# Windowed attention and a gated MLP in one kernel: a new order for all steps, with GpSimd's loads placed anew

## The chip, the cores and the metric

The kernel runs on one core of a Trainium2 chip. The metric is the time of one execution in device microseconds; "before" is the median of three runs. An engine is named as the profile names it: PE (TensorE's matmuls, with PEld for its weight loads), DVE (VectorE), ACT (ScalarE), POOL (GpSimd), SP (SyncE). SPq and POOLq are the instructions with which SP and POOL start DMA transfers.

## What is computed

Two stages, one behind the other. The first is attention with a sliding window of 128 and four "sink" positions that every query sees; the second is a gMLP block over its result. Shapes: batch 4, 8 heads, sequence 768, head size 64; model width 512, hidden width 1024 (two halves of 512).

```
scores = q @ k^T / 8                               # per batch and head
keep   = (col < 4) | (0 <= row - col < 128)
a      = softmax(where(keep, scores, -1e9))
x      = (a @ v), heads side by side               # [4, 768, 512]
h      = gelu_tanh(x @ w_in);  u, v = halves of h
v_n    = (v - mean) / sqrt(var + 1e-6) * g_ln
v_s    = w_sg @ v_n (over the sequence) + b_sg
out    = x + (u * v_s) @ w_out                     # float32
```

## The kernel before

The four batches go through one after the other, and the attention of one batch is interleaved with the gMLP of the batch before it. Everything is cut into named steps, some 670 of them, and the string STEPS lists them in the order in which they are issued. Each engine, and each of the two DMA queues (SP's and POOL's), carries out its own instructions in exactly that order. A step waits only for the data and the buffers that it needs; so the list fixes, for every engine, who stands behind whom. The numbers behind a step's name are batch, head pair or tile group; a last letter D, A or P says which engine does the step (DVE, ACT, POOL).

The steps that matter here:

- **Loads of q, k, v.** Batch 0's q and k come by head pairs as float32 over SP's queue (LPQ, LPK: four pairs each, 393 KB each), are cast to bf16 by an engine (CPQ, CPK), and are transposed on PE (TQ, TK: 12 transposes each), with the result copied out of PSUM by EQ and EK. Batches 1 and 2 are loaded over POOL's queue with a cast in the DMA (LQ, LK, six tiles each, 128 KB as bf16) and transposed on PE as well; batch 3 is loaded the same way, but its transposes are DMA transposes on SP's queue (DQ, DK). v is loaded over POOL's queue in two halves of four heads (LVH, 384 KB as bf16 each). w_in comes in two halves (LW.0 for the v half, LW.1 for the u half, 512 KB as bf16), w_sg in two (LWS), w_out in one (LWO), all over POOL's queue.
- **Attention.** QK.b.p.g makes the scores of head pair p for two tiles of queries (g = 0, 1, 2; a fourth number means that the mask is added on PE with two more matmuls), EX takes exp on ACT, MK applies the mask (on DVE in one instruction, on POOL in two), SK and SX do the sink columns. AV.b.p.k multiplies with v, where batch 0 has k = 0, 1, 2 (two tiles each) and the others k = 0, 1 (three tiles each). NR divides by the row sums and writes x (x_sb).
- **gMLP.** x is transposed, for batch 0 on PE (XT, copied out by XE), for the others by DMA transposes on SP's queue (XD, half a batch each). MV is the v half of x @ w_in (8 matmuls of 512 columns), GV its gelu on ACT; MU and GU are the same for the u half. BN, RS, NM and Z are the normalization (RS, a power of -1/2, on POOL). WT and WE transpose w_sg once. SP is the product with w_sg (SP.b.hf.dc, six matmuls), GT scales and adds the bias, GM multiplies with u. OU is the product with w_out, RA adds x, ST and SH store over SP's queue. The very last tile goes in two column halves (OH, RH, SH).
- **Buffers.** PSUM has two score buffers (sc, used by QK, MV and MU in the order of the list) and four others (mm, used by TQ, TK, XT, AV, WT, SP, OU and so on). A step that takes a new buffer waits until the one that it used last (two or four allocations ago) has been read out.
- **Fillers.** HM.n puts n matmuls on zeros in front of the next step. TBL.E and TBL.G run an exp or a gelu on one column, so that ACT's table is loaded at that place rather than with the first real use.

Of the kernel before, what the change touches and what calls it, by code (L numbers as in the profile page):

```python
# [30 lines left out]
LK.1.4 NM.0.1 WE.0.A WT.1 GV.0.2 LK.1.5 TK.1.1 MU.0.2 LB.P EK.1.1.A BN.0.2 Z.0.0.A LK.2.0 WT.2 GU.0.2 MU.0.0 WE.1.D
RS.0.2 WE.2.D Z.0.1.A LQ.2.0 NM.0.2 Z.0.2.A Z.0.3.D Z.0.4.D WT.3 LQ.2.1 WT.4 GU.0.0 TBL.E WE.3.D WT.5 LQ.1.4 Z.0.5.D
TQ.1.1 QK.1.0.0 EQ.1.1.D QK.1.1.0 LQ.1.5 SP.0.0.0 WE.4.D LK.2.1 EX.1.0.0 VSM.1 SP.0.0.1 WE.5.D EX.1.1.0 LVH.1.0
GT.0.0.0 TK.1.2 KS.1 GT.0.0.1 QK.1.2.0 QK.1.3.0 EX.1.2.0 SP.0.0.2 LVH.1.1 GM.0.0.0.D EX.1.3.0 MK.1.2.0.D TQ.2.0
EK.1.2.A LQ.2.2 QK.1.0.1 EQ.2.0.D QK.1.1.1 TQ.1.2 EX.1.0.1 GT.0.0.2 LWO SP.0.0.3 EQ.1.2.D EX.1.1.1 LK.2.2 MK.1.0.1.D
TK.2.0 MK.1.0.0.D QK.1.2.1 LK.2.3 EK.2.0.A QK.1.3.1 MK.1.3.0.D SK.1.0 GM.0.0.1.D LQ.2.3 SP.0.1.0 EX.1.2.1 GT.0.0.3
MK.1.1.0.D LQ.2.4 EX.1.3.1 SP.0.1.1 MK.1.1.1.D LQ.2.5 MK.1.2.1.D SX.1.0 QK.1.0.2 QK.1.1.2 GT.0.1.0 EX.1.0.2 GM.0.0.2.P
SP.0.1.2 GT.0.1.1 EX.1.1.2 LK.2.4 GM.0.1.0.D AV.1.0.0 MK.1.3.1.D AV.1.1.0 LK.2.5 GM.0.0.3.D QK.1.2.2 GT.0.1.2 QK.1.3.2
EX.1.2.2 SP.0.1.3 NR.1.0.0 MK.1.1.2.P EX.1.3.2 NR.1.1.0 AV.1.2.0 AV.1.3.0 MK.1.0.2.P GT.0.1.3 QK.2.0.0 QK.2.1.0
NR.1.2.0 EX.2.0.0 OU.0.0 MK.1.2.2.P NR.1.3.0 TK.2.1 RA.0.0 AV.1.0.1 XD.1.0 EK.2.1.A MK.1.3.2.P AV.1.1.1 NR.1.0.1  # L40
AV.1.2.1 EX.2.1.0 GM.0.1.2.P NR.1.1.1 AV.1.3.1 NR.1.2.1 QK.2.2.0 LK.3.0 QK.2.3.0 EX.2.2.0 OU.0.1 NR.1.3.1 GM.0.1.3.P
EX.2.3.0 TBL.G OU.0.2 XD.1.1 RA.0.1 GM.0.1.1.P TK.2.2 MK.2.3.0.D TQ.2.1 LVH.2.0 TQ.2.2 EQ.2.1.D MV.1.0 EQ.2.2.D LQ.3.0
EK.2.2.D LQ.3.1 VSM.2 MU.1.0 GV.1.0 MK.2.1.0.D LVH.2.1 BN.1.0 MV.1.1 GU.1.0 LQ.3.2 RA.0.2 LQ.3.3 MK.2.0.0.D MV.1.2
GV.1.1 MK.2.2.0.D LK.3.1 KS.2 LK.3.2 BN.1.1 MU.1.1 GV.1.2 LK.3.3 BN.1.2 RS.1.1 MU.1.2 GU.1.1 LQ.3.4 NM.1.1 Z.1.0.A
RS.1.2 OU.0.3 GU.1.2 TBL.E LQ.3.5 NM.1.2 Z.1.1.D SK.2.0 Z.1.4.D QK.2.0.1 Z.1.2.D Z.1.3.A QK.2.1.1 Z.1.5.D OU.0.4
RA.0.3 DK.3.0 SP.1.0.0 RA.0.4 SX.2.0 EX.2.0.1 SP.1.0.1 GT.1.0.0 DQ.3.0 EX.2.1.1 GM.1.0.0.D SP.1.1.0 MK.2.0.1.P
GT.1.0.1 QK.2.2.1 ST.0.3 GT.1.1.0 QK.2.3.1 GM.1.0.1.P DQ.3.1 EX.2.2.1 AV.2.0.0 SP.1.1.1 MK.2.1.1.D EX.2.3.1 MK.2.2.1.P
NR.2.0.0 AV.2.1.0 QK.2.0.2 DQ.3.2 QK.2.1.2 KS.3 EX.2.0.2 MK.2.3.1.P NR.2.1.0 SP.1.1.2 GT.1.1.1 EX.2.1.2 OU.0.5
MK.2.0.2.P GT.1.1.2 ST.0.0 ST.0.4 QK.2.2.2 RA.0.5 QK.2.3.2 MK.2.1.2.P EX.2.2.2 AV.2.2.0 AV.2.3.0 NR.2.2.0 SP.1.1.3
EX.2.3.2 NR.2.3.0 QK.3.0.0 MK.2.3.2.P QK.3.1.0 GT.1.1.3 XD.2.0 EX.3.0.0 AV.2.0.1 MK.2.2.2.D AV.2.1.1 EX.3.1.0 NR.2.0.1  # L50
AV.2.2.1 GM.1.1.3.P ST.0.1 NR.2.1.1 AV.2.3.1 ST.0.2 ST.0.5 GM.1.1.0.P SK.3.0 NR.2.2.1 QK.3.2.0 QK.3.3.0 NR.2.3.1
EX.3.2.0 GM.1.1.2.P SP.1.0.2 EX.3.3.0 XD.2.1 SP.1.0.3 GT.1.0.2 SX.3.0 TBL.G MK.3.3.0.D MV.2.0 GM.1.0.2.P DK.3.1
GM.1.1.1.D LK.3.4 MK.3.0.0.D OU.1.3 LVH.3.0 GV.2.0 OU.1.4 RA.1.3 LVH.3.1 OU.1.5 ST.1.3 RA.1.4 GT.1.0.3 MV.2.1 ST.1.4
MK.3.1.0.D LK.3.5 BN.2.0 GM.1.0.3.P MV.2.2 GV.2.1 BN.2.1 MU.2.1 GV.2.2 BN.2.2 RS.2.1 MU.2.0 GU.2.1 NM.2.1 RA.1.5
RS.2.2 MU.2.2 GU.2.0 NM.2.2 Z.2.4.D Z.2.5.D Z.2.0.A Z.2.1.D OU.1.0 GU.2.2 TBL.E Z.2.2.D MK.3.2.0.D OU.1.1 RA.1.0
Z.2.3.D QK.3.0.1 QK.3.1.1 RA.1.1 SP.2.0.0 EX.3.0.1 DK.3.2 EX.3.1.1 OU.1.2 MK.3.0.1.P GT.2.0.0 ST.1.5 VSM.3 ST.1.0
QK.3.2.1 ST.1.1 QK.3.3.1 EX.3.2.1 SP.2.1.0 GM.2.0.0.D MK.3.1.1.P RA.1.2 EX.3.3.1 SP.2.0.1 ST.1.2 MK.3.3.1.P QK.3.0.2
GT.2.0.1 QK.3.1.2 EX.3.0.2 SP.2.1.1 GT.2.1.0 MK.3.2.1.P EX.3.1.2 GM.2.1.0.D SP.2.1.2 GT.2.1.1 GM.2.0.1.D AV.3.0.0
MK.3.1.2.P GT.2.1.2 AV.3.1.0 NR.3.0.0 AV.3.2.0 AV.3.3.0 MK.3.0.2.P NR.3.1.0 QK.3.2.2 QK.3.3.2 EX.3.2.2 SP.2.0.2
NR.3.2.0 NR.3.3.0 EX.3.3.2 TBL.G SP.2.0.3 MK.3.2.2.P GT.2.0.2 XD.3.0 AV.3.0.1 GT.2.0.3 MK.3.3.2.P AV.3.1.1 NR.3.0.1  # L60
AV.3.2.1 GM.2.0.3.P NR.3.1.1 AV.3.3.1 SP.2.1.3 GM.2.0.2.D GM.2.1.1.P NR.3.2.1 OU.2.0 NR.3.3.1 GT.2.1.3 XD.3.1 OU.2.1
RA.2.0 GM.2.1.3.P OU.2.2 GM.2.1.2.D SH.2.0.0 SH.2.0.1 RA.2.1 MV.3.0 RA.2.2 SH.2.1.0 SH.2.1.1 OU.2.3 GV.3.0 OU.2.4
BN.3.0 MV.3.1 RA.2.3 RA.2.4 MV.3.2 SH.2.3.0 SH.2.3.1 GV.3.1 SH.2.2.0 SH.2.2.1 SH.2.4.0 SH.2.4.1 BN.3.1 OU.2.5 GV.3.2
MU.3.2 BN.3.2 RS.3.1 MU.3.1 GU.3.2 NM.3.1 RS.3.2 NM.3.2 Z.3.0.D Z.3.1.A MU.3.0 Z.3.2.D Z.3.3.A Z.3.4.A Z.3.5.D RA.2.5
SH.2.5.0 SH.2.5.1 SP.3.1.0 GU.3.0 SP.3.1.1 GU.3.1 GT.3.1.0 SP.3.1.2 GM.3.1.0.D GT.3.1.1 SP.3.1.3 GM.3.1.1.D GT.3.1.2
# [650 lines left out]
```

## Time and profile before

| | |
|---|---|
| median of 3 runs | 155.65 us (155.44 to 155.72) |
| the profiled execution's own time | 155.89 us |
| its span, first to last instruction | 154.2 us |
| PE / DVE / ACT / POOL busy | 145.7 / 122.9 / 100.0 / 99.7 us |
| software DMA queue (POOL's) | 64608 packets, 11.01 MB, 95.7% of 16 engines' span |
| hardware DMA queue (SP's) | 22552 packets, 13.41 MB, 33.0% |
| granted TensorE clock | 1.0 throughout |

Times in the views are microseconds from the start of the span. A PE that is shown busy need not be at its peak, since matmuls are pipelined and their ends are modelled. The share of a DMA queue adds up its packets' times, and packets of one engine overlap, so a share can pass 100% in a short window. Packets and bytes per microsecond say more.

### The profile page before, as it was taken

What the parts mean: (1) busy time and instruction counts of PE and PEld (TensorE: products, weight loads), DVE (VectorE), ACT (ScalarE), POOL (GpSimd) and SP (SyncE); (2) the same over time, 40 slices, a digit from 0 to 9 for tenths busy, and PEclk for the clock granted to TensorE, in tenths of its full rate; (3) what the DMA queues carried; (4) which work ended last, traced back from release to release, by engine and by line L of the source; (5) the groups of instructions that cost most, each with busy time, mean ns of one, the idle gap of its engine ahead of it and who ended that gap; (6) DMA issues with size and microseconds to landing.
All of it is one profiled execution on the core that took longest, in us unless ns stands there. A gap on an engine that the chain in (4) does not pass through costs nothing.

```text
span 154.2 us, 3867 instructions
## 1 busy us (share of the span) xinstructions
PE 145.7 (95%) x1540; PEld 94.5 (61%) x1554; DVE 122.9 (80%) x296; ACT 100.0 (65%) x117; POOL 99.7 (65%) x127
## 2 busy tenths in 40 slices
...
GB/s 158 305 351 157 154 195 204 166 189 211 148 141 154 185 155 140 147 150 156 156 223 250 81 276 177 185 190 81 211 72 1 105 221 73 150 54 20 0 203 206
DMA packets 87178, 24.67 MB, mean 160 GB/s; under 512 B 78772, under 2 KB 84920, under 8 KB 87160
## 3 DMA queue, kind: packets, MB, share of 16 engines
q0 software_dynamic: 64608, 11.01, 95.7%
q1 hardware_dynamic: 22552, 13.41, 33.0%
...
## 4 chain that ended last, share of the span: by engine, by line
PE 54%; POOL 18%; DMA 15%; ACT 4%; DVE 4%; issue 2%; SPq 1%; DVEq 0%; ACTq 0%; POOLq 0%
PE mm L627 15%; DMA v_sb<-in_v_dram 11%; PE mm L644 10%; PE sc L566 9%; PE sc L607 8%; POOL q L225 5%; POOL k L225 4%; DMA uT<-in_k_dram 4%; PE sc L483 4%; PE mm L524 3%; POOL v_sb L271 3%; PE mm L528 2%; POOL wsg_gated L637 2%; POOL P L498 2%; POOL P L501 2%
## 5 line engine op out<-in xcount | busy, mean ns | idle before, releaser
L488 ACT ACTIVATE P<-sc 128x1024 bf16<-128x1024 f32 (+1 forms) x48 | 43.4, 952 | 10.3 <-PE sc L483 10.1
L627 PE MATMUL mm<-wsgT,z 128*128 128x384 bf16 x192 | 34.4, 327 | 0.3 <-ACT z L597 0.3
L627 PEld LDWEIGHTS <-z 128*128 128x128 bf16 x192 | 17.6, 98 | 12.5 <-issue 0.7
L570 ACT ACTIVATE vt<-sc 128x1024 f32<-128x1024 f32 x12 | 12.3, 1027 | 18.4 <-PE sc L566 18.4
L632 DVE SCALAR_TENSOR_TENSOR gtmp<-mm,g_sb,b_bc 128x384 bf16<-128x384 f32 x32 | 19.0, 610 | 4.2 <-PE mm L627 4.0
L637 POOL TENSOR_TENSOR wsg_gated<-gtmp,uT 128x384 bf16<-128x384 bf16 x15 | 14.9, 1006 | 11.3 <-DVE gtmp L632 11.2
L607 PE MATMUL sc<-xT,w_in_sb 128*128 128x256 bf16 x192 | 22.1, 273 | 0.0
L566 PE MATMUL sc<-w_in_sb,xT 128*128 128x512 bf16 x92 | 21.8, 379 | 0.2
L644 PE MATMUL mm<-w_out_sb,wsg_gated 128*128 128x512 bf16 x85 | 21.2, 379 | 0.5
L498 POOL TENSOR_SCALAR_AFFINE_SELECT P<-P 128x512 bf16<-128x512 bf16 x21 | 13.7, 653 | 11.4 <-ACT P L488 11.4
L607 PEld LDWEIGHTS <-w_in_sb 128*128 128x128 bf16 x192 | 18.7, 98 | 2.9
L579 DVE BATCH_NORM_STATS2 st<-vt 128x6 f32<-128x512 f32 x24 | 15.4, 685 | 6.1 <-ACT vt L570 6.0
L541 DVE TENSOR_TENSOR x_sb<-mm,rcp 128x384 bf16<-128x384 f32 (+1 forms) x36 | 18.5, 513 | 1.2
L588 POOL TENSOR_TENSOR rs<-rs,neg_half 128x4 f32<-128x4 f32 (+1 forms) x8 | 7.1, 882 | 15.8 <-DVE rs L583 14.4
L225 POOL DMA_DIRECT2D k<-in_k_dram x18 | 16.4, 924 | 1.3 <-DMA v_sb<-in_v_dram 1.3
L648 DVE TENSOR_TENSOR ot<-mm,x_sb 128x512 f32<-128x512 f32 x23 | 15.4, 683 | 2.2 <-PE mm L644 2.2
L225 POOL DMA_DIRECT2D q<-in_q_dram x18 | 16.8, 956 | 0.0
L524 PE MATMUL mm<-v_sb,P 128*128 128x65 bf16 x192 | 16.1, 194 | 0.6 <-DVE x_sb L541 0.4
L524 PEld LDWEIGHTS <-P 128*128 128x128 bf16 x192 | 14.5, 97 | 2.5 <-DMA v_sb<-in_v_dram 0.6
L528 PE MATMUL mm<-v_sb,P 128*128 128x65 bf16 x160 | 15.4, 193 | 0.4 <-POOL P L501 0.4
L612 ACT ACTIVATE uT<-sc 128x1024 bf16<-128x1024 f32 x12 | 12.2, 1024 | 5.1 <-PE sc L607 5.1
L566 PEld LDWEIGHTS <-xT 128*128 128x128 bf16 x96 | 9.2, 98 | 10.1
...
## 6 DMA issues: line engine op xcount, KB each, us to landing
...
```

Of the source, the lines that this page charges most:

```text
L225: return nc.gpsimd.dma_start(out=dst.rearrange("p (h d) -> p h d", h=H), in_=heads(src, b, i))
L488: nc.scalar.activation(out=P.new((b, p, g))[:, :, 0:w], in_=sc_ring[b, p, g][:, :, 0:w], func=AF.Exp, scale=scale)
L498: nc.gpsimd.affine_select(out=p4[:, :, :, 0:128], in_=p4[:, :, :, 0:128], compare_op=ALU.is_ge, fill=0.0, base=0, pattern=[[0, 2], [0, 2], ...
L524: nc.tensor.matmul(av[:, il, hl, :], pt[:, hl, c:c + 128], vb[:, h, i, :], start=first, stop=False)
L528: nc.tensor.matmul(av[:, il, hl, :], pt[:, hl, c:c + 128], vb[:, h, i - 1, :], start=False, stop=(i < 2 and il == n - 1 and hl == 1))
L541: nc.vector.tensor_mul(x_sb.get(b)[:, i0:i0 + n, 128 * p:128 * (p + 1)].rearrange("p t (h d) -> p t h d", h=2), av[:, :, :, 0:Dh], rcp[:, ...
L566: nc.tensor.matmul(hp[:, jl, :], xT[b][:, 2 * g + jl, c, :], w_in_sb[:, c, d_half:2 * d_half], start=(c == 0), stop=(c == KD - 1))
L607: nc.tensor.matmul(hp[:, dc // 2, 256 * (dc % 2):256 * (dc % 2 + 1)], w_in_sb[:, c, 128 * dc:128 * (dc + 1)], xT[b][:, 2 * g:2 * g + 2, c, :],
L627: nc.tensor.matmul(ps[:, 0:NH], z[b][:, si, 128 * dc:128 * (dc + 1)], wsgT[:, si, NH * hf:NH * (hf + 1)], start=(si == 0), stop=(si == NT ...
L632: nc.vector.scalar_tensor_tensor(out=gtmp.new((b, hf, dc)), in0=mm_ring["g", b, hf, dc][:, 0:NH], scalar=g_sb[:, dc:dc + 1], in1=b_bc[:, N ...
L637: (nc.vector if e == "D" else nc.gpsimd).tensor_mul(gated(b, hf)[:, dc, :], gtmp[b, hf, dc], uT[b][:, dc, NH * hf:NH * (hf + 1)])
L644: nc.tensor.matmul(ps, gated(b, hf)[:, dc, 128 * tl:128 * (tl + 1)], w_out_sb[:, dc, :], start=(dc == 0), stop=(dc == KU - 1))
```

## The change

STEPS is written in a new order from its first step to its last. The steps are the same, with these exceptions and notes:

- Some steps change the engine. From ACT to DVE go CPQ.0, CPK.2, XE.0.1, XE.0.2, EK.0.1, EK.0.3, EK.1.0, EK.1.1, EK.1.2, EK.2.1, EQ.0.2, WE.0 and a few Z; from DVE to ACT EQ.0.0, EQ.0.1, EQ.0.3, EQ.1.2, GCP, WE.1 and some Z; CPK.1 goes from POOL to DVE and CPQ.3 from DVE to POOL; masks and GM steps are dealt anew between DVE and POOL (MK.0.2.2 and MK.0.3.2 go to POOL).
- On POOL's queue, v of batch 0 is issued behind the masks' set-up, in front of all casts; then come two q tiles of batch 1 and both halves of w_in (with CPQ.3.P between the halves), half of w_sg, and then the rest.
- The order of the pair loads on SP's queue becomes q0, k0, k1, q1, q2, q3, k2, k3.
- Fillers: 19 matmuls instead of 21.
- TBL gets a second argument that it doesn't use; its seven calls stand in other places (TBL.G.2 in front of EX.2.2.0; TBL.E.1 and TBL.E.2 behind the first exps of their stretch; TBL.G.3, TBL.E.3 and TBL.G.4 at the end).
- OH.3.5.1 is issued before OH.3.5.0, for which OH takes its buffer with whichever half comes first.

The start of the list, where most of the prediction's steps lie:

```diff
-WARM LPQ.0 FILL LPK.0 LPK.1 LPQ.1 LPQ.2 LG MASK LPK.2 LPK.3 CPQ.0.A VSK LPQ.3 IDEN CPK.0.A IDEN2 MASK0 HM.9 TQ.0.0
-TK.0.0 EQ.0.0.D EK.0.0.A VSO HM.4 QK.0.0.0 ZERO CPK.1.P QK.0.0.1.1 EX.0.0.0 LVH.0.0 EX.0.0.1 QK.0.0.2.1 CPQ.1.D TK.0.1
-EX.0.0.2 LC CPQ.2.D LVH.0.1 TQ.0.1 MK.0.0.0.D EK.0.1.A HM.1 TQ.0.2 EQ.0.1.D EQ.0.2.A HM.3 QK.0.1.0 CPK.2.A CPK.3.P
-QK.0.1.1.1 EX.0.1.0 LQ.1.0 CPQ.3.D TK.0.2 EX.0.1.1 TK.0.3 EK.0.2.D LQ.1.1 TQ.0.3 EK.0.3.A GTR EQ.0.3.D LW.0 HM.1
-QK.0.2.0 QK.0.2.1 EX.0.2.0 LK.1.0 KS.0 VSM.0 HM.3 SK.0.2 EX.0.2.1 SK.0.1 MK.0.2.0.D AV.0.0.0 LW.1 QK.0.3.0.1
...
-MK.0.1.2.P QK.0.3.2 AV.0.3.1 EQ.1.0.A NR.0.2.1 XT.0.0 NR.0.3.1 LWS.0 AV.0.0.2 EX.0.3.2 TBL.G AV.0.1.2 XE.0.0.D LK.1.1
-XT.0.1 MK.0.2.2.D MV.0.0 XE.0.1.A LK.1.2 NR.0.0.2 MK.0.3.2.D LK.1.3 NR.0.1.2 AV.0.2.2 AV.0.3.2 LQ.1.2 NR.0.2.2 GV.0.0
...
+WARM ZERO FILL IDEN MASK LPQ.0 LPK.0 MASK0 CPQ.0.D LPK.1 LVH.0.0 IDEN2 LVH.0.1 CPK.1.D CPK.0.A LPQ.1 HM.7 TQ.0.0 HM.3
+TK.0.0 EQ.0.0.A EK.0.0.A HM.4 QK.0.0.0 LPQ.2 LPQ.3 TK.0.1 LQ.1.0 LQ.1.1 LG LW.0 QK.0.0.1.1 CPQ.1.D EK.0.1.D CPQ.2.D
+TQ.0.1 EX.0.0.0 VSK EX.0.0.1 EQ.0.1.A CPQ.3.P QK.0.0.2.1 LPK.2 LW.1 LPK.3 EX.0.0.2 VSO LWS.0 MK.0.0.0.D CPK.3.P
+QK.0.1.1.1 TQ.0.2 CPK.2.D EQ.0.2.D QK.0.1.0 EX.0.1.1 TK.0.2 TQ.0.3 EX.0.1.0 LC LK.1.3 TK.0.3 EK.0.2.D QK.0.2.0
+EQ.0.3.A EX.0.2.0 QK.0.2.1 EX.0.2.1 EK.0.3.D KS.0 MK.0.1.0.D HM.3 SK.0.1 SX.0.1 VSM.0 QK.0.3.0.1 QK.0.3.1 EX.0.3.0
+EX.0.3.1 MK.0.3.1.P SK.0.2 HM.1 AV.0.1.0 AV.0.1.1 AV.0.0.1 MK.0.2.1.D QK.0.1.2 MK.0.2.0.D NR.0.1.0 QK.0.3.2 SX.0.2
+AV.0.0.0 GTR NR.0.1.1 EX.0.1.2 GCP.A NR.0.0.1 HM.1 AV.0.3.0 AV.0.2.1 NR.0.0.0 NR.0.3.0 MK.0.1.2.P NR.0.2.1 QK.0.2.2
+AV.0.2.0 AV.0.3.1 EX.0.3.2 AV.0.0.2 NR.0.2.0 NR.0.3.1 TQ.1.0 NR.0.0.2 EX.0.2.2 XT.0.0 MK.0.3.2.P MK.0.2.2.P XT.0.1
+XE.0.0.D EQ.1.0.A XE.0.1.D AV.0.1.2 NR.0.1.2 AV.0.3.2 LK.1.1 AV.0.2.2 MV.0.0 MV.0.1 TBL.G.1 NR.0.3.2 LK.1.0 GV.0.0
```

And the places of the later batches that the prediction speaks of, as they stand in the new list:

```
MK.1.3.2.P LK.3.0 LQ.2.5 GM.0.1.2.P EX.2.0.0 QK.2.1.0 NR.1.0.1 GM.0.1.0.P NR.1.2.0 LVH.2.0 NR.1.3.0 OU.0.0 AV.1.2.1
RA.0.0 AV.1.1.1 NR.1.2.1 EX.2.1.0 OU.0.1 AV.1.3.1 QK.2.2.0 NR.1.1.1 RA.0.1 LQ.3.1 LQ.3.0 QK.2.3.0 LQ.3.4 XD.1.0
GM.0.1.1.D GM.0.1.3.D TK.2.2 NR.1.3.1 MK.2.1.0.D TQ.2.1 OU.0.2 TBL.G.2 EX.2.2.0 EK.2.2.D LQ.3.5 TK.2.1 LK.3.1 XD.1.1
RA.0.2 EX.2.3.0 VSM.2 MV.1.0 GV.1.0 MU.1.0 EK.2.1.D MK.2.2.0.D BN.1.0 MV.1.1 GU.1.0 LQ.3.3 DK.3.0 MK.2.0.0.D MV.1.2
...
MK.2.3.1.D AV.2.2.0 AV.2.0.0 LK.3.3 GT.1.1.0 NR.2.2.0 NR.2.0.0 GM.1.1.0.P MK.2.1.2.P AV.2.1.0 SP.1.1.2 AV.2.3.0
...
GM.1.1.2.P ST.0.0 NR.2.3.1 XD.2.0 QK.3.3.0 EX.3.2.0 SP.1.0.3 EX.3.3.0 MV.2.0 OU.1.3 XD.2.1 MV.2.1 GT.1.0.2 GV.2.0
...
GT.3.0.0 GM.3.1.1.P GT.3.1.3 SP.3.1.2 GT.3.1.2 GM.3.1.2.D SH.2.0.0 GM.3.1.3.D GM.3.0.3.P SH.2.5.1 SP.3.0.1 GM.3.0.0.P
OU.3.3 GT.3.0.1 GM.3.0.1.D SH.2.4.1 RA.3.3 OU.3.4 RA.3.4 OU.3.0 ST.3.3 OU.3.1 TBL.G.3 TBL.E.3 OU.3.2 RA.3.0 OH.3.5.1
RA.3.1 OH.3.5.0 ST.3.4 RA.3.2 RH.3.5.0 RH.3.5.1 ST.3.0 ST.3.1 ST.3.2 SH.3.5.0 SH.3.5.1 TBL.G.4
```

```diff
-    def TBL(func):
+    def TBL(func, turn):
...
-        ps = mm_ring["o", b, t] if h else fresh(mm_ring, ("o", b, t))
+        ps = mm_ring["o", b, t] if ("o", b, t) in mm_ring.held else fresh(mm_ring, ("o", b, t))
```

More of the change, by code (lines that the diff above doesn't have):

```diff
@@ L26 @@
-MK.0.1.0.D SX.0.1 SX.0.2 QK.0.3.1 MK.0.2.1.P GCP.D NR.0.0.0 EX.0.3.0 AV.0.0.1 AV.0.1.0 AV.0.1.1 NR.0.0.1 EX.0.3.1
-QK.0.1.2 NR.0.1.0 AV.0.2.0 AV.0.3.0 EX.0.1.2 MK.0.3.1.P NR.0.1.1 QK.0.2.2 AV.0.2.1 NR.0.2.0 EX.0.2.2 TQ.1.0 NR.0.3.0
-MK.0.1.2.P QK.0.3.2 AV.0.3.1 EQ.1.0.A NR.0.2.1 XT.0.0 NR.0.3.1 LWS.0 AV.0.0.2 EX.0.3.2 TBL.G AV.0.1.2 XE.0.0.D LK.1.1
-XT.0.1 MK.0.2.2.D MV.0.0 XE.0.1.A LK.1.2 NR.0.0.2 MK.0.3.2.D LK.1.3 NR.0.1.2 AV.0.2.2 AV.0.3.2 LQ.1.2 NR.0.2.2 GV.0.0
-MV.0.1 NR.0.3.2 LQ.1.3 BN.0.0 LWS.1 XT.0.2 GV.0.1 MU.0.1 XE.0.2.A BN.0.1 WT.0 GU.0.1 TK.1.0 MV.0.2 RS.0.1 EK.1.0.A
@@ L31 @@
[L31 to L65, printed above, removed]
@@ L66 @@
-SP.3.0.0 GM.3.1.2.D SP.3.0.1 GT.3.0.0 GT.3.1.3 SP.3.0.2 GT.3.0.1 GM.3.1.3.P SP.3.0.3 GM.3.0.0.D GM.3.0.1.P GT.3.0.2
-OU.3.3 GM.3.0.2.D GT.3.0.3 OU.3.4 GM.3.0.3.D RA.3.3 OU.3.0 RA.3.4 ST.3.3 OU.3.1 RA.3.0 ST.3.4 OU.3.2 ST.3.0 RA.3.1
-OH.3.5.0 OH.3.5.1 ST.3.1 RA.3.2 ST.3.2 RH.3.5.0 SH.3.5.0 RH.3.5.1 SH.3.5.1
+WARM ZERO FILL IDEN MASK LPQ.0 LPK.0 MASK0 CPQ.0.D LPK.1 LVH.0.0 IDEN2 LVH.0.1 CPK.1.D CPK.0.A LPQ.1 HM.7 TQ.0.0 HM.3
+TK.0.0 EQ.0.0.A EK.0.0.A HM.4 QK.0.0.0 LPQ.2 LPQ.3 TK.0.1 LQ.1.0 LQ.1.1 LG LW.0 QK.0.0.1.1 CPQ.1.D EK.0.1.D CPQ.2.D
@@ new lines @@
+AV.0.2.0 AV.0.3.1 EX.0.3.2 AV.0.0.2 NR.0.2.0 NR.0.3.1 TQ.1.0 NR.0.0.2 EX.0.2.2 XT.0.0 MK.0.3.2.P MK.0.2.2.P XT.0.1
+XE.0.0.D EQ.1.0.A XE.0.1.D AV.0.1.2 NR.0.1.2 AV.0.3.2 LK.1.1 AV.0.2.2 MV.0.0 MV.0.1 TBL.G.1 NR.0.3.2 LK.1.0 GV.0.0
+LK.1.2 NR.0.2.2 XT.0.2 MU.0.1 LWS.1 VSM.1 GV.0.1 LQ.1.3 GU.0.1 BN.0.0 XE.0.2.D MV.0.2 WT.0 MU.0.2 BN.0.1 WE.0.D GV.0.2
+LQ.1.2 LB.P TK.1.0 RS.0.1 LQ.1.5 NM.0.1 BN.0.2 WT.1 Z.0.3.A LQ.2.0 LK.1.4 Z.0.2.A MU.0.0 Z.0.1.D WT.2 WT.3 EK.1.0.D
+Z.0.0.D RS.0.2 GU.0.2 TK.1.1 QK.1.0.0 NM.0.2 Z.0.4.D WE.2.D Z.0.5.D LQ.2.1 LQ.1.4 WE.1.A KS.1 GU.0.0 WE.3.D QK.1.1.0
```

27 lines of the change are left out of this document (added).

## The prediction

> **What bounds the kernel now.** I read the busy times by stage first, then the DMA queues, then the timeline of the stage that the change rebuilds most.
>
> The windows, in microseconds from the span's start: length, then busy time of each engine.
>
> ```profile
> 0.00:16.50 16.50, 14.05 (x165) 7.01 (x169) 10.20 (x31) 12.41 (x15) 10.47 (x19) 1.00 1.36 236
> ...
> 23.40:76.00 52.60, 51.29 (x568) 36.01 (x571) 43.49 (x107) 41.64 (x50) 46.65 (x53) 1.00 2.01 165
> 76.00:150.50 74.50, 73.92 (x674) 46.14 (x678) 62.65 (x139) 39.35 (x45) 36.58 (x47) 1.00 0.74 136
> ```
>
> From 23.4 us (the first matmul of MV.0.0 starts at 23.45) to 150.5 PE is busy 125.2 of 127.1 us, at full clock. So a new order can win at most the 1.9 us of idle time there. What comes before, the start, is different: there PE does little that isn't filler, waiting for q, k and v. So the question is when MV.0.0 starts after the change, and whether the rest stays as dense.
>
> The DMA queues in chosen windows (packets, MB, packet time as a share of 16 engines). The first is 6 to 10.5 us, where only SP's loads of the q and k pairs run; then 11.4 to 21.5, where GpSimd's queue (software) runs nearly alone.
>
> ```profile
> q1 hardware_dynamic: 1182, 1.71, 104.6%
> ...
> q0 software_dynamic: 9000, 1.57, 236.6%
> q1 hardware_dynamic: 129, 0.07, 2.7%
> ```
>
> Alone, SP's queue moves 1.71 / 4.5 = 380 GB/s. The 1.57 MB of the second window are exactly v of batch 0, two q tiles and the first half of w_in (2x384 + 2x128 + 512 KB): 10.1 us. The two hardly overlap before, because POOL reaches the loads of v only after its cast of k pair 1:
>
> ```profile
> 7.69 0.83 POOL L204 TENSOR_SCALAR k<-uT 128x768 bf16<-128x768 f32 x1 [4.17 <-DMA uT<-in_k_dram]
> 8.48 3.26 POOL L271 DMA_DIRECT2D v_sb<-in_v_dram  x2
> 11.83 0.83 POOL L204 TENSOR_SCALAR k<-z 128x768 bf16<-128x768 f32 x1
> ```
>
> The last k pair is therefore there by 11.8 (the second cast starts without a wait). What happens when both queues are full shows at 97.5 to 100, where two stores run beside loads of v; below it the software queue alone (102 to 104) and stores alone (108 to 110).
>
> ```profile
> q0 software_dynamic: 2036, 0.26, 165.7%
> q1 hardware_dynamic: 139, 0.25, 31.7%
> ...
> q0 software_dynamic: 2464, 0.31, 245.5%
> ...
> q1 hardware_dynamic: 461, 0.76, 102.6%
> ```
>
> Software packets: 814 per us against 1232 alone, 66%. SP's queue: 0.25/2.5 = 100 GB/s against 380, 26%.
>
> **The change, part by part.** *The start.* The new order takes the cast of k pair 1 from POOL to DVE and puts v's two loads right behind MASK on POOL, and behind them LQ.1.0, LQ.1.1 and LW.0; nothing on POOL waits until CPQ.3.P. MASK waits for the mask's memset on DVE, now behind ZERO (0.5 us later than before): it ends at about 3.1, the loads are issued from 3.1 (1.83 us for the first, as at 8.48), and the first software packet follows some 1.1 us behind that (11.4 against 10.3 before): 6.0 us. By 6.0 SP's queue has moved 1.17 MB of the eight pairs' 3.15 (the DMA view of 1 to 6 us); 1.98 MB are left, now beside a software queue full for 10.1/0.66 = 15.3 us, to 21.3. At 26 to 33% of 380 GB/s (the 33% is that of a transpose beside loads at 58 to 59: 0.08 MB in 1 us against 0.24 alone) that is 16 to 20 us, so the last pair, k 3, lands at 21.3 to 23, not at 11.8. Bounds: 11.8 if SP's queue goes first, 23 if it gets 26% throughout. I take 21.5, by the nearest row: about where the software queue runs dry, since POOL waits in CPQ.3.P for q pair 3 before it issues LW.1.
>
> [...]
>
> From k 3's landing L to MV.0.0 in the new order, by rows of before: CPK.3.P 0.1 + 0.83; transposes TK.0.3 0.6; QK.0.2.0, which stands behind it on PE, 0.35. Then ACT is the chain: EX.0.2.0 0.71, EX.0.2.1 0.92, SX.0.1 0.3, EX.0.3.0 0.71, EX.0.3.1 0.92, SX.0.2 0.39, EX.0.1.2 0.92, GCP.A 0.2, EX.0.3.2 1.03 (its end), together 6.1 us. Behind it MK.0.3.2 and MK.0.2.2, both moved to POOL, 2 x 1.24, then AV.0.2.2 0.4: MV.0.0 now stands behind all AV steps of batch 0, where before two of them followed it. Sum L + 10.9 = 32.4 against 23.45: +8.95. The two AV steps (0.36 each) no longer follow: -0.72. What covered this before was that all pairs had landed before v's loads began.
>
> *Later loads.* POOL issues LK.1.1 and those behind it only after MK.0.2.2.P, at about L + 10.6. TK.1.0, the first to need them, comes 9.5 us of PE work behind MV.0.0, and two such loads take POOL 1.8 us to issue and land some 7 us after (median on the page 6.5 and 7.3): nothing, with under 1 us of cover; and the wait for k at 55 us (0.4) goes.
>
> *Table loads.* TBL.G.2 stands ahead of EX.2.2.0, so ACT loads gelu, exp again and gelu again: 2 x 1.28 + 0.2 more between EX.2.1.0 and GV.1.0. ACT sits idle 1.33 and 2.03 us there before. In the new order PE has 7.8 us of work from QK.2.0.0's end to MV.1.0's end (QK 0.54, OU 3 x 0.86, AV 3 x 0.54, transposes 3 x 0.45, MV 1.73); ACT needs four EX (3.0), three loads (3.84) and the touch (0.2), 7.0, before GV.1.0 can start: nothing, with 0.8 us of cover left; past that each us of ACT is one of PE, for MU.1.0 and MV.1.1 wait for sc's two slots. TBL.G.3, E.3 and G.4 run behind the last gelu, beside PE's last 13 us: nothing.
>
> *Between batches.* XD.1.0 to XD.3.1 keep their queue, with stores now behind some of them. Following mm's ring of four: SP.1.1.2 waits for GT.1.1.0, behind two masks and GM.1.0.0 on DVE, 1.0. MV.2.1 follows MV.2.0 with one OU between instead of three; XD.2.1 needs 4 us from NR.2.3.1, so 0.6. OU.3.3 comes one SP behind its last GT, 0.4. Gone: the k wait above, the z wait (0.3) at SP.1.0.0, since no table load stands before that batch's Z on ACT, and 0.4 for P. Net +0.9, bounds -1.9 (no idle left) and +3.5 (each DVE lag of this kind whole).
>
> *Tail.* OH.3.5.0 now comes last and both RH follow it in order: 0.42 more (L661).
>
> Sum against the profiled execution: 155.89 + 8.95 - 0.72 + 0.9 + 0.42 = 165.4. That execution is 0.24 above the median of the three runs, so 165.2; rounded 165.0.
>
> **Rivals.**
> (a) The queues share evenly: 190 GB/s, L = 6.0 + 10.4 = 16.4, MV.0.0 at 27.3, 160.1. For it: some engines ran the last pair packets back to back until 12.2 with software packets about. Against: both mixed windows.
> (b) The pairs hold their places and L stays 11.8. Then ACT decides, one us behind from QK.0.0.1 (it now waits for TK.0.1 and so for k 1): EX.0.2.2 ends at 22.6, POOL's two masks bring MV.0.0 to 24.8, +1.35; 155.65 + 1.35 - 0.72 + 0.9 + 0.42 = 157.6. For it: SP has issued all eight loads by 6.4, before software packets come.
> (c) Faster: v is no longer late. The chain of waits before runs through its load, and the first AV starts 0.04 us behind it:
>
> ```profile
> 8.48 8.04 DMA v_sb<-in_v_dram
> ```
>
> With v there by 14 and the pairs in their places, L + 10.9 brings MV.0.0 at 22.7 if ACT keeps up with its copies gone to DVE, and without new waits behind it that is 155.65 - 0.75 - 0.72 + 0.42 = 154.6. It decides only up to L = 12. Against: the mixed windows, and that DVE, busy 43.5 of 52.6 us, is given ACT's copies.
> (d) The change doesn't do what it says: keeping loads and transposes apart buys nothing, because POOL still issues LVH.2.0 to LQ.3.4 around XD.1.0, and PE doesn't wait for xT before. That alone would be 155.7.
>
> **How the numbers follow.** Forecast 0.60, its own range 162.5 to 167.5 (L from 20.5 to 23, the waits' bounds in part); (a) 0.17; (b) 0.14; (c) 0.06; a wash near 155.7 0.03. Eight in ten: from 157.3, which takes in (a) and most of (b), to 167.0. About 0.2% is what a measurement of this kernel can tell from no change (the three runs lie 0.28 us apart). Faster 0.07 ((c) and the low end of (b)), same 0.03, slower 0.90.
>
> **What would show it.** Software packets from about 6 us beside q1 packets up to 21; q1 near 100 GB/s there; POOL's cast of k 3 (L204) waiting for DMA up to 21 us, and MV.0.0 (L566) first at about 32; PE idle or on filler before. From MV.0.0 to the last matmul 127 us, as before. 11 table loads beside the first. Wrong if the last k pair lands before 15 us, if MV.0.0 starts before 27, or if PE is over 4 us idle behind it.

## The result, and the profile after

The changed kernel takes 163.73 us (median of four runs: 162.25, 162.28, 165.18, 167.06) against 155.69 for the kernel before. The runs at 165.18 and 167.06 had a lower granted clock (0.987 and 0.979) and are left out of the ratio, 1.042 (95% interval 1.0381 to 1.0459): **slower**, as forecast. The profiled execution took 162.25 with a span of 160.6 us, 6.4 longer than before.

The windows of the changed kernel (length, busy time of PE, PEld, DVE, ACT, POOL, granted clock, DMA share, GB/s):

```profile
0.00:16.50 16.50, 12.72 (x141) 6.27 (x142) 11.08 (x29) 8.79 (x11) 12.18 (x20) 1.00 1.25 232
16.50:30.00 13.50, 13.01 (x202) 9.22 (x205) 12.34 (x36) 11.11 (x16) 8.99 (x13) 1.00 1.81 185
30.00:84.00 54.00, 49.04 (x542) 34.40 (x545) 47.68 (x106) 38.80 (x43) 44.25 (x51) 1.00 1.87 153
84.00:156.80 72.80, 71.69 (x662) 44.67 (x662) 57.45 (x131) 41.58 (x48) 35.92 (x44) 1.00 0.74 128
```

MV.0.0 starts at 26.26 instead of 23.45, so the start costs 2.8 us. The rest has lost its density: PE stands idle for 5.0 us between 30 and 84. The waits of PE (us in total, times, longest) name the holes:

```profile
PE sc L566 <- DMA xT<-x_sb: 3.2, 1, 3.2
PE mm L376 <- DVE iden L315: 2.2, 1, 2.2
...
PE mm L382 <- DVE x_sb L541: 0.9, 1, 0.9
PE sc L483 <- DMA kT<-k: 0.8, 1, 0.8
```

**The start.** DVE's copy of the identity and POOL's steps in the changed kernel's timeline:

```profile
5.40 1.15 DVE L315 CAST iden<-iden 128x128 bf16<-128x128 f32 x1
...
3.08 3.45 POOL L271 DMA_DIRECT2D v_sb<-in_v_dram  x2
...
13.82 0.92 POOL L204 TENSOR_SCALAR k<-z 128x768 bf16<-128x768 f32 x1 [0.44 <-DMA z<-in_k_dram]
```

The identity takes 1.15 us (0.23 before) and ends at 6.55, within 0.02 us of the end of POOL's issue of v's loads (6.53); the first transposes start at 6.60, not at 4.89. That POOL's issue holds the copy up is a guess from the two ends. In loads_back (this and the next are experiments below), which issues the loads later, PE's wait for the identity falls from 2.2 us to 0.6; but in v_early_zero the same copy takes 0.23 us at 3.5, with POOL's issue of v's loads running from 3.46 to 6.55, and a pair cast of the kernel before took only 0.56 us at 8.68, beside POOL's issue of v's loads (8.48 to 11.74). The last pair is there by 13.82, where the forecast had 21.5. The DMA queues from 6 to 10.5 us, and then beside XD.1.1 (67.5 to 70; packets, MB, share):

```profile
q1 hardware_dynamic: 1038, 1.49, 97.4%
q0 software_dynamic: 332, 0.04, 14.3%
...
q0 software_dynamic: 1033, 0.13, 80.1%
q1 hardware_dynamic: 1032, 0.26, 80.0%
```

Issued at 3.08, v's packets come only from 8.54 on (5.5 us behind the issue; 2.6 before), so until then the pairs are alone. From 9 to 12 us 202 software packets of 128 bytes pass per us beside 181 pair packets of 1536: nearly one to one. Alone, the pairs make 239 (6.5 to 8.5) to 260 (8.5 to 10.5 in the kernel before), so they keep 70 to 75%.

**PE's speed at the start.** In after it is not the last pair that sets MV.0.0. ACT, which does the exps, has no pause of over 0.1 us from 12.23 to 24.1, and this chain starts late. x_first (one of the experiments below) has the same list up to MV.0.0, and the same rows earlier; after's stand first:

```profile
7.39 1.46 PE L190 MATMUL mm<-warm 128*128 128x512 bf16 x3
12.23 1.02 ACT L488 ACTIVATE P<-sc 128x1024 bf16<-128x1024 f32 x1 [0.51 <-PE sc L483]
...
7.06 0.82 PE L190 MATMUL mm<-warm 128*128 128x512 bf16 x3
10.94 1.02 ACT L488 ACTIVATE P<-sc 128x1024 bf16<-128x1024 f32 x1 [0.51 <-PE sc L483]
```

The PE rows are the same three filler matmuls, at about half speed in after. The column of the granted clock reads 1.00 there in both, so at the start it can't be relied on. Six kernels have this start unchanged:

| kernel | three fillers ahead of TK.0.0 | four ahead of QK.0.0.0 | MV.0.0 |
|---|---|---|---|
| x_first | 0.82 | 1.04 | 25.13 |
| dk_first | 0.82 | 1.04 | 25.69 |
| after | 1.46 | 1.04 | 26.26 |
| fill | 1.46 | 1.06 | 26.28 |
| start_new | 1.46 | 1.89 | 27.52 |
| loads_late | 1.46 | 1.89 | 27.65 |

The later PE comes to full speed, the later MV.0.0 starts. So 0.6 to 1.1 of the 2.8 us in after go with PE's speed, which differs from run to run. The new start has seven fillers in front instead of nine, and PE then idles 2.2 us for the identity; that this is why PE comes to speed late is not shown.

**Transposes beside loads.** The second block above shows one to one again: 1033 packets to 1032. A transpose moves 256 bytes per packet, alone at 822 per us (61 to 62 us), here at 413. The chain of waits through it:

```profile
61.81 2.02 DVE wsg_gated L637 x2
...
64.55 8.10 DMA xT<-x_sb
72.65 0.05 issue
72.69 2.55 PE sc L566 x11
```

MV.1.1's last four matmuls could have begun at 69.5; they wait until 72.65 for XD.1.1, whose 1536 packets run from 66.86 to 71.42. On SP's queue 32 small packets (4 bytes) follow at 71.65 to 72.17, the first 0.23 us behind the last of the 1536; why only then is not shown. In front of XD.1.1 NR.1.3.1 stands on DVE behind two GM steps that take 2.1 us; POOL runs two of its own GM at the same time (61.69 to 63.61).

### The profile page after: what moved, and what is told of

The parts are those of the page before. It is cut to its first block, busy times and chain, and to the rows that moved or that the text cites. A ratio compares the mean times of both kernels' runs of the same rounds, so it can differ in the third digit from the quotient of the medians.

```text
span 160.6 us, 3855 instructions
## 1 busy us (share of the span) xinstructions
PE 146.5 (91%) x1539; PEld 94.6 (59%) x1552; DVE 129.3 (81%) x301; ACT 100.3 (62%) x116; POOL 101.3 (63%) x126
## 4 chain that ended last, share of the span: by engine, by line
PE 44%; DVE 11%; DMA 10%; issue 1%; ACT 1%; POOL 0%; SPq 0%; DVEq 0%
PE mm L627 13%; PE sc L566 8%; PE mm L644 8%; PE sc L607 7%; DMA xT<-x_sb 5%; DMA kT<-k 5%; DVE x_sb L541 3%; PE sc L483 3%; PE mm L524 2%; DVE P L495 2%; DVE wsg_gated L637 2%; PE mm L528 2%; DVE ot L648 1%; DVE gtmp L632 1%; PE mm L531 1%
## 5 line engine op out<-in xcount | busy, mean ns | idle before, releaser
L488 ACT ACTIVATE P<-sc 128x1024 bf16<-128x1024 f32 (+1 forms) x48 | 43.5, 952 | 14.0 <-PE sc L483 13.8
L627 PEld LDWEIGHTS <-z 128*128 128x128 bf16 x192 | 17.8, 98 | 11.7 <-issue 0.8
L498 POOL TENSOR_SCALAR_AFFINE_SELECT P<-P 128x512 bf16<-128x512 bf16 x20 | 13.2, 660 | 15.1 <-ACT P L488 11.6
L570 ACT ACTIVATE vt<-sc 128x1024 f32<-128x1024 f32 x12 | 12.3, 1024 | 15.3 <-PE sc L566 14.5
L588 POOL TENSOR_TENSOR rs<-rs,neg_half 128x4 f32<-128x4 f32 (+1 forms) x8 | 7.6, 949 | 22.2 <-DVE rs L583 21.5
L648 DVE TENSOR_TENSOR ot<-mm,x_sb 128x512 f32<-128x512 f32 x23 | 15.3, 683 | 2.9 <-PE mm L644 1.7
L495 DVE TENSOR_TENSOR P<-P,mask 128x768 bf16<-128x768 bf16 (+1 forms) x24 | 16.3, 693 | 0.0
L225 POOL DMA_DIRECT2D q<-in_q_dram x18 | 16.3, 911 | 0.0
L524 PE MATMUL mm<-v_sb,P 128*128 128x65 bf16 x192 | 16.0, 194 | 0.1
L483 PE MATMUL sc<-qT,kT 64*128 64x128 bf16 (+1 forms) x256 | 14.5, 238 | 1.3 <-DMA kT<-k 0.8
## 6 DMA issues: line engine op xcount, KB each, us to landing
wsg_gated<-in_moe_w_sg_dram POOLq DMA_DIRECT2D x2, 576.0 KB, 11.7
```

The lines of the kernel that those rows point to most:

```text
L225: return nc.gpsimd.dma_start(out=dst.rearrange("p (h d) -> p h d", h=H), in_=heads(src, b, i))
L483: nc.tensor.matmul(sc[:, hl, c:c + 128 * ni], at(kT, b)[rows, j, p, :], at(qT, b)[rows, i:i + ni, p, :], start=not biased, stop=(not biase ...
L488: nc.scalar.activation(out=P.new((b, p, g))[:, :, 0:w], in_=sc_ring[b, p, g][:, :, 0:w], func=AF.Exp, scale=scale)
L495: nc.vector.tensor_mul(pt[:, :, 0:w], pt[:, :, 0:w], m.unsqueeze(1).to_broadcast([128, 2, w]))
L524: nc.tensor.matmul(av[:, il, hl, :], pt[:, hl, c:c + 128], vb[:, h, i, :], start=first, stop=False)
L627: nc.tensor.matmul(ps[:, 0:NH], z[b][:, si, 128 * dc:128 * (dc + 1)], wsgT[:, si, NH * hf:NH * (hf + 1)], start=(si == 0), stop=(si == NT ...
```

## The experiments

Each is an edit of STEPS; "after" is the changed kernel. Ratios are to the kernel before, with 95% intervals.

### Where is the loss: start or rest?

**start_new**: the new list up to MV.0.0, then what is left in the old order.

> The new list up to MV.0.0, then the old list's remaining steps in the old order. If the two parts of the new list cost what the traces put on them, this carries the start alone: MV.0.0 at 26.3 us and 155.7 + 2.8 - 0.7 = 157.8 us, without a wait of MV.1.1 for xT. If the start only costs because what follows was fitted to it (or the reverse), it lies above 159 or below 156.5.

Measured: 158.14 us, 1.0125 [1.0049, 1.0201]. MV.0.0 at 27.52, and no wait of PE for xT.

**rest_new**: the old list up to MV.0.0, then what is left in the new order.

> The old list up to MV.0.0, then the new list's remaining steps in the new order. By the traces' account: MV.0.0 at 23.5, the waits behind it as in the changed kernel (about 4.2 us more than before, 3.1 of them MV.1.1 waiting for the second half of xT), so 155.7 + 4.2 = 159.9 us. If the waits behind MV.0.0 came from the late start, 157 or less.

Measured: 155.69 us, 0.9979 [0.9947, 1.001]. MV.0.0 at 23.45. The new rest alone costs nothing: MV.1.1 runs at 64.97 without a wait, although NR.1.3.1 stands behind the same two GM steps. Here DVE is all but through with them when POOL starts its own two; in after all four run at once (rest_new first, then after):

```profile
59.31 0.62 DVE L637 TENSOR_TENSOR wsg_gated<-gtmp,uT 128x384 bf16<-128x384 bf16 x2
59.88 2.13 POOL L637 TENSOR_TENSOR wsg_gated<-gtmp,uT 128x384 bf16<-128x384 bf16 x2
...
61.73 2.10 DVE L637 TENSOR_TENSOR wsg_gated<-gtmp,uT 128x384 bf16<-128x384 bf16 x2
61.69 1.92 POOL L637 TENSOR_TENSOR wsg_gated<-gtmp,uT 128x384 bf16<-128x384 bf16 x2
```

With 0.62 us instead of 2.10, after would have issued XD.1.1 at about 63.1 (an estimate from these rows), ahead of LVH.2.0 at 63.56. No run isolates this. One hole is left in rest_new, that of QK.3.1.2:

```profile
PE sc L483 <- DMA kT<-k: 0.7, 1, 0.7
```

So neither half has the wait for xT, but the whole has it. It is made by the two together: start_new's 2.2 us (158.14 against 155.99 beside it) and rest_new's nothing do not add up to 6.4.

### The start

**v_early_zero**: the kernel before with the disputed part alone, the five loads put early. (ZERO, memsets on DVE, has to stand ahead of v's loads, whose tiles it writes too.)

```diff
-WARM LPQ.0 FILL LPK.0 ... IDEN2 MASK0 HM.9 ... ZERO CPK.1.P ... LVH.0.0 ... LVH.0.1 ... LQ.1.0 ... LQ.1.1 ... LW.0
+WARM LPQ.0 FILL ZERO LPK.0 ... IDEN2 MASK0 LVH.0.0 LVH.0.1 LQ.1.0 LQ.1.1 LW.0 HM.9 ... CPK.1.D ...
```

> As v_early (the kernel before, with v's two loads, LQ.1.0, LQ.1.1 and LW.0 on GpSimd right behind the identity and the cast of k pair 1 on DVE), but with ZERO, which writes the ones column of v's tiles, moved up behind FILL on DVE as in the changed kernel; in v_early it stood behind the loads, had to wait for v to land and held CPK.1.D until 19.9 us. Step of the prediction that is tested (the pairs get a third of their rate beside the loads, the last one at 21.5): MV.0.0 near 32, 163 or more. Theory B (turns packet by packet, pairs 1 us late): the packets of the pairs end by 13.8, cast of k pair 3 starts by 13.0, MV.0.0 at 24.0 to 25.2, time 156.2 to 157.5. Rival (v there early is worth more than that): MV.0.0 by 23.4, 155.7 or less.

Measured: 156.11 us, 1.0024 [0.9991, 1.0057]. MV.0.0 at 23.59, 0.14 later than before. POOL in its timeline:

```profile
3.46 3.09 POOL L271 DMA_DIRECT2D v_sb<-in_v_dram  x2
...
12.48 0.83 POOL L204 TENSOR_SCALAR k<-z 128x768 bf16<-128x768 f32 x1 [3.43 <-DMA z<-in_k_dram]
```

k pair 3 is cast at 12.48 instead of 11.83, so it is 0.65 us late, and the chain behind it hides most of that. So of the 8.95 us that the prediction's main step gave to these loads, they cost 0.1. Theory B's pairs about 1 us late fit, but it put their price too high: the interval takes in no change at all. One to one is not the rule throughout here: from 9 to 10 us 585 software packets pass beside 118 of pairs, and only from 10.5 to 12 are they 198 to 179 per us. Why is open.

**v_early** was the same without ZERO's move.

> The kernel before with one thing of the change: v's two loads, LQ.1.0, LQ.1.1 and LW.0 on GpSimd right behind the identity (issued from 3.5 us instead of 8.5), and for that the cast of k pair 1 on DVE. Nothing else moves. Step of the prediction that is tested (loads on GpSimd beside the pairs cost the pairs their bandwidth; last pair at 21.5, MV.0.0 at 32): 163 or more. Theory B (the queues take turns packet by packet, the pairs keep some 70% of their rate and land about 1 us later): last pair at 13.0 to 13.8 instead of 12.3, MV.0.0 at 24.0 to 25.0 instead of 23.45, time 156.2 to 157.4. Rival (v there early is worth more than the pairs lose): MV.0.0 at 23.3 or earlier, 155.7 or less.

Measured: 167.54 us, 1.0741 [1.0685, 1.0798]. ZERO, behind v's loads in the list, waited for v to land, and CPK.1.D behind it on DVE; so the time says nothing of the pairs. k pair 3 is cast at 12.57 here too. What it shows is the granted clock behind a long idle time (third column from the right; 1.00 before 10 us):

```profile
PE mm L376 <- DVE k L200: 11.0, 1, 11.0
...
10.00:15.00 5.00, 0.00 (x0) 0.00 (x0) 0.00 (x0) 0.49 (x1) 2.43 (x3) 0.63 1.80 229
15.00:20.00 5.00, 0.00 (x0) 0.00 (x0) 0.31 (x5) 0.00 (x0) 0.07 (x1) 0.50 2.54 165
20.00:25.00 5.00, 4.53 (x44) 2.38 (x44) 3.24 (x6) 2.33 (x3) 0.00 (x0) 0.51 1.37 186
```

**iden_first**: after, with the identity's copy and CPQ.0.D ahead of MASK0 on DVE, so that the copy is done before POOL issues loads.

> The changed kernel with IDEN2 and CPQ.0.D ahead of MASK0 on DVE; the loads stay early, nothing else moves. If the late first transposes (6.6 us) set the start, they come at about 5 and MV.0.0 1 to 1.6 us earlier: 160.7 to 161.3. If the last pair's landing at 13.4 and what hangs on it set it, MV.0.0 stays within 0.3 us of 26.3 and the time is 162.0 to 162.3.

Measured: 160.17 to 166.0 us, median 164.55; the profiled execution (163.97) has PE at half clock from 73.35 to 76.76, so no ratio is given. The first transposes start at 5.14, 1.5 us earlier, but MV.0.0 only at 25.67. PE is at full speed by then, and x_first and dk_first, at full speed with the late identity, have 25.13 and 25.69: from the earlier copy no gain can be told. k pair 3 is cast at 14.76 here.

**loads_back**: after, with the five early loads behind CPQ.3.P on POOL.

> The changed kernel (162.26 in its undisturbed runs) with one move: the two loads of v, two of q and the first half of w_in go behind CPQ.3.P on POOL. Theory A, POOL's issue of loads holds DVE up: the cast of the identity (L315, 1.15 us, ended with the issue of v's second load) takes 0.2 to 0.3 again, the first transposes start at about 5.2 instead of 6.6, and MV.0.0 moves up by 1.2 to 2 us: 160.3 to 161. Theory B, the pair loads lose to the software queue on the DMA engines: the last pair lands 1.1 us earlier (12.3), MV.0.0 gains about that, L315 stays at 1.15 or so, 161.2. If neither matters, 162.3, or later because v is late.

Measured: 169.42 us, 1.0832 [1.0715, 1.0949]. The wait for the identity fell to 0.6 as theory A said. But CPK.3.P now stood behind seven load issues on POOL and came at 19.0:

```profile
PE mm L376 <- POOL k L204: 4.8, 1, 4.8
```

**start_mend** puts CPK.1 back on POOL and the loads of q and w_in behind CPK.3.P.

> The changed kernel with the start's GpSimd order put as in the kernel before: the cast of k pair 1 back on GpSimd and ahead of v's two loads, and the loads of q tiles 0 and 1 and of w_in (LQ.1.0, LQ.1.1, LW.0, LW.1) behind the cast of k pair 3. Theory A (the loads issued from 3.1 us on hold DVE's first steps and take DMA turns from the pairs): DVE's identity copy takes 0.2 us again instead of 1.15, the first transposes start at about 5.0 instead of 6.6, the last pair is there by 12.3 instead of 13.4, and MV.0.0 starts at 23.6 to 24.6 instead of 26.26: 159.9 to 160.6. Rival (the start is late by its order on ACT and DVE, one transpose behind another, not by the loads): MV.0.0 at 25.5 or later, 161.5 or more. A new wait is possible: w_in's first half is asked for later and could hold MV.0.0.

Measured: 165.11 us, 1.0587 [1.0517, 1.0658]. First transposes at 5.02, but MV.0.0 at 26.88, later than theory A has it. PE's waits in the start, and DVE's way to the longer one:

```profile
PE mm L376 <- DVE k L200: 2.2, 1, 2.2
...
PE mm L376 <- POOL k L204: 1.0, 1, 1.0
...
12.77 0.89 DVE L354 CAST v_sink<-headsel 128x8 bf16<-128x8 f32 x2 [1.56 <-POOL headsel L343]
...
14.02 1.57 DVE L200 CAST k<-z 128x768 bf16<-128x768 f32 x1
```

The 1.0 us are for the cast of k pair 1 (8.13), which waited for its load. The 2.2 us are for that of k pair 2, and here the edit made a wait of its own: DVE stood for headsel, which POOL makes behind v's loads, and these are issued at 8.91 now instead of 3.08. So the run doesn't decide between theory A and its rival; with iden_first it shows that early first transposes alone don't bring MV.0.0 forward.

In all kernels with the new start's order CPK.3.P begins at 13.8 to 14.8 (apart from loads_back), with the old one at 11.7 to 12.6. One pair is 256 packets; at 181 per us that is 1.4 us, the price of q 3 going ahead of k 2 and k 3 on SP's queue. That the order of the pairs makes k 3 late is argued from these times; a kernel with only that order undone was not run.

### The wait for xT

**x_first**: after, with one step moved.

```diff
-GM.0.1.1.D GM.0.1.3.D TK.2.2 NR.1.3.1 MK.2.1.0.D
+NR.1.3.1 GM.0.1.1.D GM.0.1.3.D TK.2.2 MK.2.1.0.D
```

> The changed kernel with one step moved: NR.1.3.1 ahead of GM.0.1.1.D and GM.0.1.3.D on DVE, so that XD.1.1 is issued about 2.2 us earlier (62.4 instead of 64.55), ahead of the issue of LVH.2.0 on GpSimd (63.56). Theory C (MV.1.1's wait of 3.2 us for xT comes from NR.1.3.1's place behind two gate copies, and from the loads that the late transpose then shares the DMA engines with): the wait falls to 0 to 0.6 us, the time by 2.4 to 3.2 us, to 159.0 to 159.9 where the changed kernel has 162.25. Rival (GpSimd's loads alone set it, whatever the place of NR.1.3.1): wait at least 2 us, time 161 to 162.

Measured: 159.57 us, 1.0257 [1.018, 1.0333]. The time is as theory C said, but MV.0.0 comes 1.1 us earlier than in after though nothing ahead of it was moved, so not all of the gain is the move's. The picture is not theory C's: MV.1.1 waits no more, but MV.1.0 now waits 2.64 us for XD.1.0:

```profile
58.71 7.20 DMA xT<-x_sb
```

XD.1.0 is released 7.2 us behind its issue, with XD.1.1 (issued 61.99) and LVH.2.0 (62.28) close behind it. Behind that wait the clock falls to half, from 66.50 to 69.92:

```profile
64.00:66.00 2.00, 0.05 (x1) 0.05 (x2) 2.00 (x4) 0.15 (x1) 2.00 (x3) 1.00 2.33 172
66.00:68.00 2.00, 2.00 (x7) 0.71 (x8) 0.19 (x1) 0.00 (x0) 2.00 (x3) 0.63 1.88 221
68.00:70.00 2.00, 2.00 (x9) 1.11 (x8) 0.00 (x0) 0.92 (x1) 2.00 (x3) 0.52 2.45 156
```

**loads_late**: after, with LVH.2.0, LVH.2.1, LK.3.1 and five q tiles behind RS.1.1 on POOL.

> The changed kernel with eight loads on GpSimd (LVH.2.0, LVH.2.1, LK.3.1 and the five q tiles around XD.1.1) moved behind RS.1.1, so that XD.1.1, issued as late as before (about 64.5), finds the DMA engines empty. Theory C: alone it takes the 2.4 to 3 us of 61 to 64 instead of 5.6, xT is there near 69.5, and MV.1.1 waits 0 to 1 us instead of 3.2: 159.5 to 160.3, unless v or q of the next batch then comes late, which would show as a wait of PE for them after 80 us. Rival (only the late issue counts): wait 2.5 us or more, no change of the time.

Measured: 169.0 us, 1.0839 [1.0775, 1.0904]. The point in question is settled: XD.1.1 is issued at 65.94, 1.4 us later than in after, and yet MV.1.1, from 69.91, doesn't wait for it. Its last packets pass at 69.2, 3.2 us behind the issue, where after needs 7.6 (72.2). So the late issue alone costs nothing; it is the sharing. The price came from elsewhere. RS.1.2 stood behind the moved loads on POOL, and the normalization of v with it:

```profile
PE mm L627 <- DVE z L600: 6.6, 1, 6.6
...
75.69 3.13 POOL L271 DMA_DIRECT2D v_sb<-in_v_dram  x2
...
79.68 5.27 POOL L225 DMA_DIRECT2D q<-in_q_dram  x6
84.90 0.79 POOL L588 TENSOR_TENSOR rs<-rs,neg_half 128x2 f32<-128x2 f32 x1
```

Laid side by side, the kernels with XD.1.1 issued ahead of LVH.2.0 have no wait for it, and all others do:

| kernel | XD.1.1 issued | LVH.2.0 issued | PE's wait for XD.1.1 |
|---|---|---|---|
| before | 59.93 | 62.32 | none |
| start_new | 62.75 | 65.15 | none |
| rest_new | 60.66 | 61.95 | none |
| rest_dk | 62.22 | 63.51 | none |
| loads_late | 65.94 | 75.69 | none |
| x_first | 61.99 | 62.28 | none (XD.1.0: 2.6) |
| after | 64.55 | 63.56 | 3.2 |
| dk_first | 63.98 | 62.99 | 4.0 |
| iden_first | 63.97 | 62.97 | 4.1 |
| start_mend | 65.17 | 64.18 | 3.7 |
| loads_back | 69.43 | 68.44 | 3.2 |
| fill | 64.58 | 63.59 | 1.2, behind 2.6 of fillers |

In rest_new the transpose leads by 1.3 us and its 1536 packets pass between two groups of loads in 2.1 us (62.10 to 64.22); in after it is 1.0 behind, and needs 4.6. The start's delay does not move all engines alike: from rest_new to after, MV.1.0 is 3.5 us later, XD.1.1 3.9 (1.5 of it the two GM steps) and LVH.2.0 only 1.6, since POOL had time to spare.

**fill**: after, with HM.12 ahead of MV.1.1.

> The changed kernel with twelve filler matmuls of 0.22 us (2.6 us of PE) ahead of MV.1.1, written into the score tile that MV.1.1 then overwrites; they lie in PE's wait for xT. Theory D (the changed kernel's own runs differ, 162.25 to 167.06, because this wait, 3 to 4 us, is sometimes long enough for TensorE's granted clock to fall behind it): granted clock at least 0.995 in every run, all runs within 1.5 us, median 161.8 to 163. Rival (clock and scatter have another origin): runs still spread over 3 us with clocks down to 0.98, median 163.5 or more.

Measured: 163.69 us, 1.0507 [1.0448, 1.0566], runs from 163.07 to 165.05. The clock is 0.995 to 1.0 in all four, so that half of theory D holds as far as four runs show it: the fillers keep it up. The times do not follow (2.0 us of spread, and all above after's 162.25 and 162.28): xT is released at 73.08 in the profiled execution, 0.4 later than in after, PE still waits 1.2 us for it behind the fillers, and 0.7 for another xT at 129.2 to 129.9. The spread that is left has another origin; PE's speed at the start, which differs from run to run, is one that the runs leave open.

### The other waits

**dk_first**: after, with DK.3.2 right behind DK.3.1 on SP's queue.

> The changed kernel with DK.3.2 moved right behind DK.3.1 on SP's queue, ahead of the stores ST.0.3 to ST.1.3 that stand in front of it. Theory: QK.3.1.2's wait of 0.8 us for kT goes, and with it 0.6 to 0.9 us of the time: 161.4 to 161.6. Rival (the stores share the engines with the transpose wherever it stands, or GT's reading of mm is late next): the wait stays or turns into one for sc or mm, under 0.3 us gained.

Measured: 164.38 us, 1.0563 [1.048, 1.0646]. From MV.2.1 to QK.3.1.2 it takes 17.34 us instead of 18.20, so the wait is gone, as expected. But the wait for xT is 4.0 here, one more of 0.9 came at 136, and the clock fell to half (73.10 to 76.51); the time is no better:

```profile
70.00:72.00 2.00, 0.00 (x0) 0.00 (x0) 0.14 (x1) 0.00 (x0) 1.14 (x1) 1.00 3.08 127
72.00:74.00 2.00, 0.96 (x3) 0.42 (x4) 0.00 (x0) 0.00 (x0) 0.00 (x0) 0.77 2.42 154
74.00:76.00 2.00, 2.00 (x7) 0.63 (x5) 0.00 (x1) 1.02 (x1) 0.00 (x0) 0.50 2.44 155
```

**rest_dk**: rest_new with the same move, where nothing covers it.

> The old order up to MV.0.0, the new order behind it (155.69 us, 0.998 of the kernel before), with DK.3.2 moved right behind DK.3.1, ahead of the stores. Theory: QK.3.1.2's wait of 0.7 us for kT goes and nothing else is late: 154.8 to 155.2, ratio 0.993 to 0.996. Rival (something as late stands next): 155.4 to 155.8, ratio over 0.996.

Measured: 155.42 us, 0.9974 [0.9951, 0.9997]. The wait for kT is gone here too (17.34 us again over that stretch, 18.14 in rest_new), and the kernel is below the kernel before by 0.3%, with 1 just outside the interval; against rest_new's 0.9979 the gain can't be told. The profiled execution had 1.6 us of waits for q pairs at its start and MV.0.0 at 24.33, so the theory's size isn't confirmed. It is ahead of both kernels, by a margin that the interval barely shows.

## Why the prediction was right, and where it was not

The side and the range held: 165.0 forecast, 157.3 to 167.0, measured 163.73. The forecast's likeliest mechanism did not, and each of the three signs that it named for being wrong came: the last k pair landed before 15 us (13.8), MV.0.0 started before 27 (26.26), and PE is over 4 us idle behind it (6.1). That the time lies near 165 is luck: the start was priced 6.1 us too high and the waits 3.3 too low, and the two errors partly cancel. PE's busy time from MV.0.0 to its last matmul, before and after:

```profile
23.45:150.50 127.05, 125.16 (x1240) 82.10 (x1248) 106.08 (x244) 80.94 (x94) 83.18 (x100) 1.00 1.26 148
...
26.26:156.84 130.58, 124.46 (x1222) 80.91 (x1229) 108.10 (x245) 82.19 (x94) 83.91 (x98) 1.00 1.24 139
```

Against the spans (154.2 and 160.6), term by term; PE's busy time stands for the AV steps, its idle time for the waits:

| term | forecast | measured |
|---|---|---|
| MV.0.0 later | +8.95 | +2.81 |
| two AV steps no longer behind MV.0.0 | -0.72 | -0.70 |
| waits between batches, net | +0.9 | +4.23 |
| tail | +0.42 | +0.06 |
| sum | +9.55 | +6.4 |

- **The step that failed** is the pairs' rate beside software loads, 26 to 33% of 380 GB/s and so L = 21.5. It was read off a window with stores of 2048 bytes beside loads, where SP's queue got one packet for about 15 of the other (139 to 2036), and carried over to pairs. Here they pass at nearly one to one, and the pairs keep 70 to 75%; in v_early_zero, with these loads alone put early, MV.0.0 is 0.14 us later, not 8.95. Packet size alone doesn't tell the two cases apart, and why the stores get so little stays open. The start of the software packets, too, came at 8.54 rather than 6.0. And the upper bound was added up loosely: at 26% for 15.3 us and the full rate behind it, its own rows give L = 22.5, not 23.
- **The chain behind the last pair** was sized well where it sets the start: L + 10.9. From the start of CPK.3.P to MV.0.0 it is 10.91 us in x_first, dk_first and iden_first. In after it is 12.44: there EX.0.2.0 comes 3.3 us behind CPK.3.P's start (17.16), against 1.7 in the other three, because ACT's chain is late by itself, as in rival (b).
- **The mis-sized term** is the waits between batches. None of the three that I named (SP.1.1.2, MV.2.1, OU.3.3) shows more than 0.2 us. What came are MV.1.1's for xT (3.2), TK.2.1's for x_sb (0.9), QK.3.1.2's for kT (0.8) and SK.1.0's for the gate (0.5), less what went (1.0). "XD.1.0 to XD.3.1 keep their queue" was true and not enough: the queue beside it decides. Rival (d)'s "PE doesn't wait for xT before" had the transposes and loads in view, and left out that XD.1.1 may lose its lead over LVH.2.0.
- **Rival (b)** (pairs keep their places, MV.0.0 at 24.8, 157.6) is nearest to the start as measured, in its mechanism too: ACT decides. It has no term for PE's half speed. With 3.2 us for xT it would give 160.8. Start_new, 158.14, is about this rival.
- **Table loads at nothing**: right. The added ones lie in ACT's idle time, and no wait of PE leads to them.
- **The tail**: 0.06 instead of 0.42; from PE's last matmul to the end of the span it is 3.71 us, 3.65 before.
